# Where the empty instruction runs, when a bank may be borrowed, and how the plan prices a fold: one change to a two-layer SSM-convolution and gated-MLP kernel

## The chip, the cores and the metric

The kernel runs on one core of one Trainium2 chip. The metric is device microseconds of one execution, taken as the median of several. The engines are called by the names of the profile: PE (TensorE, matrix products), PEld (its weight loads), ACT (ScalarE), DVE (VectorE), POOL (GpSimd) and SP (SyncE, which issues DMAs).

## The reference, cut to what matters

```python
x = A_q                                            # 1 x 2048 x 576, bf16
x = x + A(layernorm(x), A_k, A_v, shift_k, ssm_k, ssm_D)
x = x + B(layernorm(x), w_gate, w_up, w_down)
x = x + A(layernorm(x), ...)                       # the same A and B again
x = x + B(layernorm(x), ...)

# A: kv = causal 4-tap convolution of k with shift_k, times v
#    y  = irfft(rfft(kv) * rfft(ssm_k))[:2048] + kv * ssm_D      (along the sequence)
#    returns q * y                                 (q is the normalised x)
# B: (gelu(x @ w_gate) * (x @ w_up)) @ w_down      (576 -> 4608 -> 576)
```

The convolution y does not depend on x, so both layers use the same y. The MLP B is run for each of the two layers and is nearly all of the arithmetic.

## The kernel before, in words

**Units and visits.** The 2048 rows are cut into 4 chunks of 512. A unit is one layer of one chunk; there are 8, in the order (layer 0, chunk 0), (0, 1), (1, 0), (1, 1), (0, 2), (0, 3), (1, 2), (1, 3), numbered 0 to 7. The 4608 features are cut into three phases of 12 tiles of 128. A visit is one unit in one phase, so there are 24, which this text numbers 0 to 23. Visits 0 to 2 belong to unit 0, 3 to 8 to units 1 and 2 in turn, 9 to 14 to units 3 and 4, 15 to 20 to 5 and 6, and 21 to 23 to unit 7.

**One visit.** First the gate and up products: 12 tiles (`gu`, L1081), each 18 matmuls of 64 weight rows by 512 columns, gate on one half of the array's rows and up on the other, so that two run side by side. Each tile is then gated into `hT`: GELU on ACT and the product on DVE, in one of two ways. Either ACT does the GELU alone and DVE multiplies straight out of the accumulator bank (L1673, L1674), or ACT also copies the up half out (L1664, L1665) and DVE multiplies two bf16 tiles (L1666); the second way frees the bank without DVE. It is taken when `hurry()` holds or convolution work for DVE is queued, and ACT is free by the plan. After the 12 tiles comes the down product (`dn`, L1735) for 4 rows of 128 tokens, two rows at a time (`two_rows`).

**Half rows and the empty instruction.** A `dn` row is accumulated into the two banks of a pair, one for each half of the 576 columns. In step 0, array rows 0 to 63 feed the first bank and 64 to 127 the second; in step 1 it is the other way round. Between the steps stands `conv.hold`: an instruction that does nothing, but is made to depend on the accumulator, so that it waits for the last matmul of step 0 and the first matmul of step 1 waits for it. It sits in ACT's instruction queue (L1110) and shows in the profile as an EVENT_SEMAPHORE. The forward and inverse transforms of the convolution (`cps`, L310) use the same two steps through `both_steps`. In `two_rows` the order by hand is: 10 features of the first row, 9 of the second, the last 2 of the first, the last 3 of the second (all step 0), then step 1 of both. The last features come late because their `hT` is late.

**Banks.** The accumulator memory is used as four double banks. Three go round in turn: `pr` hands out the next to each gate/up tile and each down row. The fourth belongs to the convolution. When it is taken, the convolution may borrow the next of the three (`conv.alt`); a row or tile that comes after then gets the bank behind it. `bank_at` holds when each is free by the plan.

**The plan.** The order on every engine is fixed when the kernel is built. A set of clocks (`t.pe`, `t.dve`, `t.act`) is advanced by constants (`C_GU`, `C_DN`, `C_FOLD` and so on). After each tile, and after every second pair of matmuls in a down product, `fill` runs what is due: step 1 of convolution transforms that were opened (`run_open`), loads, additions of finished rows (`late`), convolution products on DVE (`run_v`, allowed up to a limit ahead of `t.pe`), and new transforms on PE (`run_p`). The convolution of chunk m ends in two `fold`s on DVE (L559, L560: four operations each), after which the inverse transform can run. Until the last row of chunk 1's y is planned (`hurry()`), transforms may also run between gate/up tiles; afterwards only inside down products.

`turn_row` (L1097) transposes a normalised row on PE when it would be late by DMA; `opened` takes a bank for a row; `evict` queues the addition of a finished row to x (L1752, L1765, L1771, L1773).

Of the kernel before, what the change touches and what calls it, by code (L numbers as in the profile page):

```python
# [22 lines left out]
HW = 288  # L23
# [5 lines left out]
C_GU, C_DN = 1.944, 0.245  # L29
# [4 lines left out]
C_P0, C_P1, C_AC = 1.28, 1.35, 0.7  # L34
C_TT, C_ST, C_BN, C_NORM, C_HT, C_GELU, C_EVA, C_EVD, C_YH = 0.74, 0.80, 0.47, 0.62, 0.615, 0.51, 0.56, 0.72, 0.7
C_HB = 0.345
C_FOLD = 0.38
C_TURN, DRAIN = 0.0, 0.35
LAG = 0.25
AHEAD = 2.0  # L40
# [94 lines left out]
class Conv:  # L135
# [177 lines left out]
    def both_steps(self, outs, terms):  # L313

        ps = self.ps()
        self.half_rows(outs(ps), terms, 0)
        self.hold(ps)
        yield
        self.half_rows(outs(ps), terms, 1)
        return ps  # L320

# [73 lines left out]
    def step(self, m, kv=None, loaded=False):  # L395
# [155 lines left out]
        def fold(sg):  # L551

            def run():
                if sg == 0:
                    w["free"] = self.acp.tile([P, 2, D], BF16, tag="ac", name="w")[:, 0, :]
                for plane in range(2):
                    a, b = z[plane, 0, sg][:], z[plane ^ sg, 1, sg][:]
                    up, down = (sg, sg + 2) if sg == 0 or plane else (sg + 2, sg)
                    nc.vector.tensor_tensor(out=w["free"], in0=a, in1=b, op=ALU.add)  # L559
                    nc.vector.tensor_tensor(out=a, in0=a, in1=b, op=ALU.subtract)  # L560
                    w[up, plane], w[down, plane], w["free"] = w["free"], a, b

                def fin(when):
                    for part in range(2):
                        mark(("z", sg, part), when + LAG)
                    if sg:
                        self.z_at[m] = when
                return fin
            return run
# [18 lines left out]
        for sg in range(2):  # L588
            self.V.append((now, 4 * C_FOLD, fold(sg)))
        ab = {}  # L590
# [141 lines left out]
    def run_p(self):  # L732
        t = self.t
        if not self.Pq:
            return False
        ready, cost, run = self.Pq[0]
        self.cur = 0 if self.ps_free[0] <= t.pe else 1
        if self.cur and ready() <= t.pe and self.ps_free[0] <= t.pe + (0.3 if self.between else 0.0):
            self.cur = 0
            t.pe = max(t.pe, self.ps_free[0])  # L740
        if ready() > t.pe or self.ps_free[self.cur] > t.pe or self.cur and (self.alt is None or self.alt_at() > t.pe):
            return False
        self.Pq.popleft()
        run = run()
        if next(run, "whole") == "whole":
            t.pe += cost
            if self.cur:
                self.borrowed(self.slot(), self.ps_free[1])
            return True
        self.ps_free[self.cur] = NEVER  # L750
        t.pe += cost / 2
        self.open.append((t.pe + DRAIN, cost / 2, run, self.cur, self.slot()))
        return True

    def run_open(self, now):
# [10 lines left out]
def ssm_geglu_kernel(ctx, tc, A_q, A_k, A_v, A_shift_k, A_ssm_k, A_ssm_D, B_x, B_w_gate, B_w_up,  # L766
                     B_w_down, out):
    nc = tc.nc
# [7 lines left out]
    FP = FT // NP  # L776
# [13 lines left out]
    t = Pace()  # L790
# [10 lines left out]
    def bank(n, name, shape=(P, 2, 512), dt=F32):  # L801
        return banks[n].tile(list(shape), dt, tag="pr", name=name)
# [12 lines left out]
    def add_late():  # L815
        ready, n, run = late.popleft()
        run()
        bank_at[n % 3] = t.on_dve(C_EVD, ready) + 0.15

    bank_at, was = [0.0] * 3, [0.0]  # L820

    def pr(name):
        while late and taken[0] - late[0][1] >= 2:
            add_late()
        taken[0] += 1
        was[0] = bank_at[taken[0] % 3]
        bank_at[taken[0] % 3] = NEVER
        return bank(turn[(taken[0] - 1) % 3], name)
# [11 lines left out]
    conv = Conv(tc, ctx, t, gwork, xtp, A_k, A_v, A_shift_k, A_ssm_k, A_ssm_D, ident,  # L840
                lambda *form: bank(turn[3], "cps", *form), ypool)
# [265 lines left out]
        conv.ps_free[0] = xn_at[ui]  # L1107
        xn_done[ui] = j + 1

    conv.hold = lambda ps: nc.scalar.keepalive_nop([nc.scalar.lower_ap(ps[:, :, 0:HW])])  # L1110
    conv.slot = lambda: taken[0] % 3
    conv.borrowed = bank_at.__setitem__
    conv.alt_at = lambda: bank_at[(taken[0] + 1) % 3]
# [66 lines left out]
    with tc.manual_schedule():  # L1180
# [6 lines left out]
        with ExitStack() as es:  # L1187
# [40 lines left out]
            ps = bank(3, "ps")  # L1228
# [3 lines left out]
            held = {}  # L1232
# [355 lines left out]
            order = plan.order({"DVE": 1.9, "ACT": 3.3, "PE": 3.0, "POOL": 3.0, "SP": 4.5})  # L1588
# [19 lines left out]
        hurry = lambda: (1, RT - 1) not in conv.y_at  # L1608
# [4 lines left out]
        for at, (wb, ph, ui, first, final) in enumerate(visits):  # L1613
# [32 lines left out]
            gone = deque([0.0] * 2, maxlen=2)  # L1646
            conv.alt = None
            for fi in range(FP):
                n, gi = divmod(wb * FP + fi, FG)
# [40 lines left out]
            def opened(j):  # L1690
                if j not in accs:
                    accs[j] = pr("dn"), taken[0]
                return accs[j]

            def row(j):
# [27 lines left out]

            def two_rows(j):

                order = ([(0, 0, fi) for fi in range(FP - 2)] + [(1, 0, fi) for fi in range(FP - 3)] +
                         [(0, 0, fi) for fi in range(FP - 2, FP)] + [(1, 0, fi) for fi in range(FP - 3, FP)] +
                         [(n, 1, fi) for n in range(2) for fi in range(FP)])
                for k, (n, step, fi) in enumerate(order):
                    acc, mine = opened(j + n)  # L1730
                    wn = wd[2 * wb + fi // WT][:, fi % WT, :]
                    lhs = hT[:, fi, (j + n) * P:(j + n + 1) * P]
                    for g in range(2):
                        r = slice((step ^ g) * HK, (step ^ g) * HK + HK)
                        nc.tensor.matmul(acc[:, g, 0:HW], lhsT=lhs[r], rhs=wn[r, g * HW:(g + 1) * HW],  # L1735
                                         start=step == 0 and fi == 0, stop=step == 1 and fi == FP - 1)
                    if step == 0 and fi == FP - 1:
                        conv.hold(acc)
                    t.pe += C_DN / 2
                    if step == 1 and fi == FP - 1:  # L1740
                        evict(j + n)
                    elif k % 2:
                        conv.alt = other
                        fill(t.pe + 1.5, True, conv.left > 0)

            def evict(j):
# [30 lines left out]

            conv.alt = other
            two_rows(0)
            if wb == NWB - 1:  # L1780
                conv.alt = None
                row(2)
                row(3)
            else:
                two_rows(2)
# [3 lines left out]
@with_exitstack  # L1789
def kernel(  # L1790
    ctx: ExitStack,
    tc: tile.TileContext,
    A_q: bass.AP,
    A_k: bass.AP,
    A_v: bass.AP,
    A_shift_k: bass.AP,
    A_ssm_k: bass.AP,
    A_ssm_D: bass.AP,
    B_x: bass.AP,
    B_w_gate: bass.AP,  # L1800
    B_w_up: bass.AP,
    B_w_down: bass.AP,
    out: bass.AP,
):
    ssm_geglu_kernel(tc, A_q, A_k, A_v, A_shift_k, A_ssm_k, A_ssm_D, B_x, B_w_gate, B_w_up,
                     B_w_down, out)
# [30 lines left out]
```

## Time and profile before

| what | value |
|---|---|
| median of 3 runs | 913.42 us (913.37 to 913.92) |
| the profiled execution | 913.37 us |
| its span, first to last instruction | 911.5 us |
| matmuls | 10451, busy 904.0 us |
| VectorE busy | 565.1 us |
| ScalarE busy | 363.2 us |
| GpSimd busy | 146.8 us |
| granted TensorE clock | 1.000 |

The profiled execution is 1.9 us longer than its span, and within 0.05 us of the median. Matmuls are pipelined: a recorded matmul is longer than the time by which it moves the next one, so a busy PE can still be losing time. In a timeline, rows that follow one another on an engine are merged: start, length, engine, line, operation, count, and in brackets the idle time before it with what ended it.

### The profile page before, as it was taken

The numbers are of one execution on the slowest core, as the hardware profiler recorded it, in microseconds if no ns is written. First come the engines' busy times: TensorE is split into PE (matmuls) and PEld (weight loads), VectorE is DVE, ScalarE is ACT, GpSimd is POOL, SyncE is SP. The second block draws the span as 40 slices with busy tenths as digits, with TensorE's granted clock in tenths as the row PEclk, the third lists the DMA queues.
The fourth block names the chain that finished last, engine by engine and source line by source line (L and its number), as shares of the span: only waits on it lengthen the run. The fifth ranks groups of instructions, "written<-read, shape, count | busy, mean of one in ns | idle before, by whom it ended". The sixth has DMA issues, their size and how long they took to land.

```text
span 911.5 us, 24246 instructions
## 1 busy us (share of the span) xinstructions
PE 904.0 (99%) x10451; PEld 600.2 (66%) x10451; DVE 565.1 (62%) x1129; ACT 363.2 (40%) x675; POOL 146.8 (16%) x311
## 2 busy tenths in 40 slices
PE   9999999999999999999999999999999999999998
PEld 7757656466576675765766757757757657667666
DVE  8888985885789886677888843553332334433332
ACT  7785445735425356354244223451121224321211
POOL 5533003220113012230023001220000002100000
PEclk9999999999999999999999999999999999999999
DMA  9999977449619604974934702772720820777630
GB/s 247 307 250 275 249 164 144 113 126 235 201 53 231 142 2 79 271 186 106 247 121 117 167 16 58 129 137 60 142 79 2 157 79 13 143 176 180 136 101 27
DMA packets 125839, 129.12 MB, mean 142 GB/s; under 512 B 40866, under 2 KB 118051, under 8 KB 125732
## 3 DMA queue, kind: packets, MB, share of 16 engines
q1 hardware_dynamic: 116706, 92.63, 47.8%
q0 software_dynamic: 8880, 34.36, 11.4%
q8 instruction: 81, 1.33, 0.6%
q10 hardware_dynamic: 146, 0.59, 0.2%
q14 instruction: 26, 0.21, 0.1%
HBM read 106.91 MB, written 11.80 MB: 130 GB/s over the span
## 4 chain that ended last, share of the span: by engine, by line
PE 94%; DVE 4%; ACT 1%; issue 1%; POOL 0%; ACTq 0%
PE gu L1081 58%; PE dn L1735 29%; PE cps L310 2%; PE ps L284 2%; DVE kvt L255 1%; PE dn L1701 1%; DVE kvt L261 1%; DVE kc L633 0%; PE ps L1317 0%; DVE hT L1666 0%; DVE cd L334 0%; PE ps L1452 0%; PE ps L1081 0%; DVE hh L633 0%; POOL rstd L1537 0%
## 5 line engine op out<-in xcount | busy, mean ns | idle before, releaser
L1081 PE MATMUL gu<-xnT,wgu 64*128 64x512 bf16 x5148 | 561.0, 376 | 1.1 <-DVE hT L1674 0.9
L1081 PEld LDWEIGHTS <-wgu 64*128 64x128 bf16 x5220 | 293.5, 94 | 262.3 <-issue 2.3
L1735 PE MATMUL dn<-wd,hT 64*128 64x288 bf16 x4512 | 294.6, 283 | 0.8 <-ACTq L1110 0.4
L1735 PEld LDWEIGHTS <-hT 64*128 64x128 bf16 x4512 | 253.3, 94 | 28.7 <-issue 1.6
L1673 ACT ACTIVATE ga<-gu 128x512 f32<-128x512 f32 x175 | 104.4, 597 | 318.9 <-PE gu L1081 312.7
L1674 DVE TENSOR_TENSOR hT<-ga,gu 128x512 bf16<-128x512 f32 x175 | 120.0, 686 | 172.5 <-ACT ga L1673 172.0
L1664 ACT ACTIVATE ga<-gu 128x512 bf16<-128x512 f32 x111 | 66.2, 597 | 148.4 <-PE gu L1081 140.6
L1666 DVE TENSOR_TENSOR hT<-ga 128x512 bf16<-128x512 bf16 x112 | 46.9, 421 | 54.7 <-ACT ga L1665 54.7
L1665 ACT CAST ga<-gu 128x512 bf16<-128x512 f32 x111 | 64.4, 580 | 0.0
L911 POOL TENSOR_SCALAR means<-s 128x1 f32<-128x1 f32 x28 | 16.9, 606 | 245.1 <-DVE x_c L1765 216.8
L1773 DVE TENSOR_TENSOR x_c<-x_c,dn 128x576 f32<-128x576 f32 x32 | 23.9, 751 | 26.3 <-PE dn L1735 26.2
L1771 DVE SCALAR_TENSOR_TENSOR x_c<-dn,means,x_c 128x576 f32<-128x576 f32 x28 | 22.8, 815 | 24.5 <-PE dn L1735 24.4
L927 POOL TENSOR_TENSOR rstd<-ve,neghalf_t 128x1 f32<-128x1 f32 x56 | 34.9, 623 | 4.7
L329 ACT ACTIVATE eo<-cps 128x576 f32<-128x576 f32 x40 | 25.6, 657 | 21.3 <-PE cps L310 16.7
L346 DVE TENSOR_TENSOR prod<-prod 128x576 bf16<-128x576 bf16 x64 | 29.3, 458 | 2.2
L1752 DVE TENSOR_TENSOR xn<-x_c,dn 128x576 bf16<-128x576 f32 x15 | 11.3, 753 | 26.0 <-PE dn L1735 23.6
L633 DVE TENSOR_TENSOR kc<-ab,cd 128x288 bf16<-128x288 f32 x64 | 25.5, 451 | 0.0
L444 POOL DMA_DIRECT2D kr<-Kd x20 | 11.0, 552 | 85.9 <-DVE prod L345 85.9
L911 POOL TENSOR_SCALAR nm<-s 128x1 f32<-128x1 f32 x28 | 7.9, 281 | 94.8 <-DVE x_c L965 94.7
L919 ACT ACTIVATE junk<-x_c,nm 128x576 bf16<-128x576 f32 x28 | 21.5, 767 | 4.0 <-POOL nm L911 3.5
L955 ACT ACTIVATE yh<-y,rstd 128x576 f32<-128x576 bf16 x28 | 21.2, 768 | 2.3 <-PE dn L1735 1.4
L449 POOL DMA_DIRECT2D hr<-Hd x32 | 17.6, 551 | 21.4 <-DVE prod L345 19.9
(180 smaller groups left out, 629.9 us busy)
## 6 DMA issues: line engine op xcount, KB each, us to landing
wgu<-in_B_w_gate_dram SPq DMA_DIRECT2D x45, 576.0 KB, 6.0
wd<-in_B_w_down_dram SPq DMA_DIRECT2D x30, 864.0 KB, 6.5
wgu<-in_B_w_up_dram SPq DMA_DIRECT2D x45, 512.0 KB, 9.0
hr<-Hd POOLq DMA_DIRECT2D x32, 288.0 KB, 4.7
kr<-Kd POOLq DMA_DIRECT2D x24, 288.0 KB, 4.5
Kd<-kc POOLq DMA_DIRECT2D x12, 288.0 KB, 5.1
k<-in_A_k_dram POOLq DMA_DIRECT2D x3, 1008.0 KB, 10.9
wgu<-in_B_w_up_dram SPq DMA_DIRECT2D x45, 64.0 KB, 7.9
```

What stands on the lines that cost most here:

```text
L329: nc.scalar.activation(out=eo[:], in_=ps[:, :, 0:HW], func=ACT.Copy, scale=scale)
L346: nc.vector.tensor_tensor(out=dst[:, cols], in0=pr[:, 0, cols], in1=pr[:, 1, cols], op=ALU.subtract if part == 0 else ALU.add)
L633: nc.vector.tensor_tensor(out=into[k][:, plane, cols], in0=a, in1=b, op=op)
L911: nc.gpsimd.tensor_scalar(out=v["nm"][:], in0=v["s"][:], scalar1=-1.0 / D, scalar2=None, op0=ALU.mult)
L927: nc.gpsimd.tensor_tensor(out=v["rstd"][:], in0=ve[:], in1=neghalf_t[:, 0:1], op=ALU.pow)
L1081: nc.tensor.matmul(cols(pair[:, s, :]), lhsT=w[r0:r0 + HK, k, gi * P:(gi + 1) * P], rhs=cols(xnT[r0:r0 + HK, blk_of[k], :]), start=(k == 0 ...
L1664: nc.scalar.activation(out=ga[:, 0, :], in_=pair[:, 0, :], func=ACT.Gelu_apprx_tanh)
L1665: nc.scalar.copy(out=ga[:, 1, :], in_=pair[:, 1, :])
L1666: nc.vector.tensor_tensor(out=hT[:, fi, :], in0=ga[:, 0, :], in1=ga[:, 1, :], op=ALU.mult)
L1673: nc.scalar.activation(out=ga[:], in_=pair[:, 0, :], func=ACT.Gelu_apprx_tanh)
L1674: nc.vector.tensor_tensor(out=hT[:, fi, :], in0=ga[:], in1=pair[:, 1, :], op=ALU.mult)
L1735: nc.tensor.matmul(acc[:, g, 0:HW], lhsT=lhs[r], rhs=wn[r, g * HW:(g + 1) * HW], start=step == 0 and fi == 0, stop=step == 1 and fi == FP - 1)
```

## The change

Seven edits, all in how the kernel is ordered; nothing of what is computed changes.

1. `hold` is no longer always in ACT's queue: it goes to DVE's when the plan's ACT clock is later than both its DVE and its PE clock. It returns the time at which the plan takes it to be done.
2. Step 1 of a convolution transform is not due before that time (`run_p` keeps the later of it and the drain time); step 1 of a down row moves the plan's PE clock to it.
3. In `two_rows`, the number of features of the second row that go ahead of the first row's last two is no longer always 9. For the first pair of rows it is worked out from the planned time of the last `hT` (0 to 9); for the second pair it is 0.
4. After `hurry()` has ended, the convolution may borrow one of the three banks only in the second pair of rows of a down product. The last visit's second pair (`row`) borrows none, as before.
5. Taking a bank for a row moves the plan's PE clock to the time when that bank is free.
6. `C_FOLD`, the planned cost of one fold operation, is 0.46 instead of 0.38.
7. `both_steps` hands the time from `hold` on to `run_p`.

```diff
-C_FOLD = 0.38
+C_FOLD = 0.46
@@ both_steps
         self.half_rows(outs(ps), terms, 0)
-        self.hold(ps)
-        yield
+        yield self.hold(ps)
         self.half_rows(outs(ps), terms, 1)
@@ run_p
-        if next(run, "whole") == "whole":
+        held = next(run, "whole")
+        if held == "whole":
...
-        self.open.append((t.pe + DRAIN, cost / 2, run, self.cur, self.slot()))
+        self.open.append((max(t.pe + DRAIN, held), cost / 2, run, self.cur, self.slot()))
@@ ssm_geglu_kernel
-    conv.hold = lambda ps: nc.scalar.keepalive_nop([nc.scalar.lower_ap(ps[:, :, 0:HW])])
+    def hold(ps):
+
+        eng = nc.scalar if t.act <= max(t.dve, t.pe) else nc.vector
+        eng.keepalive_nop([eng.lower_ap(ps[:, :, 0:HW])])
+        return min(t.act, max(t.dve, t.pe)) + 0.15
+    conv.hold = hold
@@ opened
                     accs[j] = pr("dn"), taken[0]
+                    t.pe = max(t.pe, was[0])
@@ two_rows
-                order = ([(0, 0, fi) for fi in range(FP - 2)] + [(1, 0, fi) for fi in range(FP - 3)] +
-                         [(0, 0, fi) for fi in range(FP - 2, FP)] + [(1, 0, fi) for fi in range(FP - 3, FP)] +
+                held = {}
+                some = math.ceil((gone[-1] + 0.5 - t.pe) * 2 / C_DN) - (FP - 1)
+                some = max(0, min(FP - 3, some)) if j == 0 else 0
+                order = ([(0, 0, fi) for fi in range(FP - 2)] + [(1, 0, fi) for fi in range(some)] +
+                         [(0, 0, fi) for fi in range(FP - 2, FP)] + [(1, 0, fi) for fi in range(some, FP)] +
                          [(n, 1, fi) for n in range(2) for fi in range(FP)])
                 for k, (n, step, fi) in enumerate(order):
                     acc, mine = opened(j + n)
+                    if step == 1 and fi == 0:
+                        t.pe = max(t.pe, held[n])
...
                     if step == 0 and fi == FP - 1:
-                        conv.hold(acc)
+                        held[n] = conv.hold(acc)
                     t.pe += C_DN / 2
                     if step == 1 and fi == FP - 1:
                         evict(j + n)
                     elif k % 2:
-                        conv.alt = other
+                        conv.alt = other if hurry() or j == 2 else None
                         fill(t.pe + 1.5, True, conv.left > 0)
```

## The prediction

> **What bounds the kernel now.** The page first: how busy each engine is.
>
> ```profile
> PE 904.0 (99%) x10451; PEld 600.2 (66%) x10451; DVE 565.1 (62%) x1129; ACT 363.2 (40%) x675; POOL 146.8 (16%) x311
> ```
>
> PE is the bound. The change removes no matmul, so all it can win is time in which PE waits. To size that I need PE's pace without waits: the chain in order of time late in the run, and a window over nine whole visits.
>
> ```profile
> 861.18 11.76 PE dn L1735 x192
> 872.94 23.31 PE gu L1081 x216
> ...
> 580.44:896.07 315.63, 315.63 (x3675) 1.00 0.50 107
> ```
>
> A visit without waits is 23.31 + 11.76 = 35.07 us, and nine of them, 315.63 us, lose nothing. So from 580 us on there is nothing to win; the visits that carry convolution work are what matters. The same rows give the unit for measuring a wait: two matmuls run side by side, so a gate/up pair takes 23.31/108 = 0.216 us and a down pair 11.76/96 = 0.1225 us; transforms (also 288 columns) are taken at the down pair's pace. A wait is then the start of a group minus the start of the group before it and its pairs. This is more than the idle time in the list of waits, because the modelled end of a matmul lies beyond the start of the next:
>
> ```profile
> PE gu L1081 <- DVE hT L1674: 0.9, 1, 0.9
> PE dn L1735 <- ACTq L1110: 0.4, 1, 0.4
> PE cps L310 <- ACTq L1110: 0.4, 1, 0.4
> PE dn L1735 <- DVE x_c L1771: 0.3, 2, 0.2
> ```
>
> Four kinds of wait, and each is named by a part of the change: a gate late behind DVE (the folds), two empty instructions (L1110), and a down row waiting for an addition to free its bank. All that PE loses in this region is small: 0.2% of 913.42 us is 1.83 us, about what a measurement of this kernel can tell from no change.
>
> **Folds priced at 0.46 (edit 6).** Visit 12, gate/up:
>
> ```profile
> 518.98 7.95 PE L1081 MATMUL gu<-xnT,wgu 64*128 64x512 bf16 x72
> 523.32 0.45 DVE L559 TENSOR_TENSOR w<-yb 128x576 bf16<-128x576 bf16 x1
> 526.76 0.46 DVE L560 TENSOR_TENSOR yb<-yb 128x576 bf16<-128x576 bf16 x1
> 527.14 2.09 DVE L1674 TENSOR_TENSOR hT<-ga,gu 128x512 bf16<-128x512 f32 x3
> 527.87 1.04 PE L1081 MATMUL gu<-xnT,wgu 64*128 64x512 bf16 x8 [0.94 <-DVE hT L1674]
> ```
>
> 36 pairs from 518.98 end at 526.75; PE goes on at 527.87: 1.12 us lost. Eight fold operations stand in front of the gate of the second tile, whose bank PE needs; they start 0.49 us apart ((526.76 - 523.32)/7) where the plan has 0.38. By the plan's constants, counted from the end of the first tile: gate at 1.67, the two shifts (0.78) to 2.45 (in the trace the tile ends 9 pairs after 518.98, at 520.92, and the first fold starts at 523.32, 2.40 later), one fold (four operations) to 3.97, the second to 5.49; the limit is C_GU + FAR = 5.54, so both go in. At 0.46 the first ends at 4.29 and the second would at 6.13: it has to wait for the next `fill`. Then convolution work is still queued, so the second tile takes the way that frees its bank from ACT, and its gate goes ahead of the second fold. At the measured 0.49 the second fold ends near 527.6, the third tile's gate 0.7 later at 528.3, and PE wants that bank at 518.98 + 5 x 1.94 = 528.7. So nothing is late next, by 0.4 us. I take -1.1; the ends are -1.12 and 0, should the folds fall elsewhere.
>
> **The empty instruction on the earlier engine, and step 1 not before it (edits 1, 2, 7).** First row, in visits 3 and 0:
>
> ```profile
> 183.63 0.82 DVE L334 TENSOR_TENSOR cd<-eo 128x288 f32<-128x288 f32 x2
> 183.64 0.65 PE L1735 MATMUL dn<-wd,hT 64*128 64x288 bf16 x8
> 184.37 0.82 DVE L633 TENSOR_TENSOR kc<-ab,cd 128x288 bf16<-128x288 f32 x2
> 184.62 0.65 ACT L329 ACTIVATE eo<-cps 128x576 f32<-128x576 f32 x1 [1.73 <-DVE cd L334]
> 184.71 0.42 PE L1735 MATMUL dn<-wd,hT 64*128 64x288 bf16 x4 [0.42 <-ACTq L1110]
> ...
> 65.12 0.74 PE L310 MATMUL cps<-ht,T 64*128 64x288 bf16 x4
> 65.69 0.42 PE L1735 MATMUL dn<-wd,hT 64*128 64x288 bf16 x4
> 66.17 0.59 ACT L1664 ACTIVATE ga<-gu 128x512 bf16<-128x512 f32 x1
> 66.49 0.30 PE L310 MATMUL cps<-ht,T 64*128 64x288 bf16 x2 [0.38 <-ACTq L1110]
> ```
>
> Visit 3: four pairs from 183.64 end at 184.13, PE goes on at 184.71: 0.58 us. The empty instruction was queued behind an eviction (L329) that itself waited for DVE to read the last one (cd). Three things now work on this: DVE may be chosen; in the first pair of rows there is one transform at a time, so evictions rarely queue; and more of the second row stands between the first row's step 0 and step 1. Ends: -0.58 and 0; I take -0.45, nearer the full wait, because any one of the three would do.
>
> Visit 0: two pairs from 65.69 end at 65.94, PE goes on at 66.49: 0.55 us, a transform's step 1 behind a GELU. Edit 2 leaves step 1 until the plan has the empty instruction done, with rows in between. The 0.33 us before it (two pairs from 65.12 end at 65.36, next at 65.69) is a borrowed bank, which edit 4 leaves alone here since `hurry()` holds. What is late next is the last gate, so I take -0.45 of ends -0.88 (both waits) and 0.
>
> Behind an empty instruction in DVE's queue stand additions and `cross` operations of the transforms; they wait until step 0 is drained. Its own execution costs nothing:
>
> ```profile
> L1110 ACTq EVENT_SEMAPHORE  x150: 17/17/17, 43.5 to 899.2; - x150
> ```
>
> **Banks, and the order of rows (edits 3, 4, 5).** Visits 4 and 9, the second pair of rows:
>
> ```profile
> 225.17 1.16 PE L1735 MATMUL dn<-wd,hT 64*128 64x288 bf16 x16
> 225.63 0.81 DVE L1771 SCALAR_TENSOR_TENSOR x_c<-dn,means,x_c 128x576 f32<-128x576 f32 x1
> 226.50 0.67 PE L1735 MATMUL dn<-wd,hT 64*128 64x288 bf16 x8 [0.17 <-DVE x_c L1771]
> ...
> 407.29 1.16 PE L1735 MATMUL dn<-wd,hT 64*128 64x288 bf16 x16
> 408.63 0.65 PE L1735 MATMUL dn<-wd,hT 64*128 64x288 bf16 x7 [0.17 <-DVE x_c L1771]
> ```
>
> Eight pairs from 225.17 end at 226.15, next 226.50: 0.35 us, and from 407.29 likewise 0.36. Row 4 opens after 10 pairs of row 3 and gets a bank whose row is still being added. In the second pair row 4 now opens after 12 pairs, 2 x 0.1225 = 0.245 us later, and with nothing borrowed in the first pair it may get an older bank. Per visit -0.245 by the order alone, -0.35 at most: I take -0.5 for both, ends -0.7 and 0. Visit 8 is the same at row 3:
>
> ```profile
> 363.95:376.39 12.44, 1.03 (x8) 0.00 (x0) 1.21 (x2) 1.00 1.20 216
> ...
> 369.71 0.75 DVE L1752 TENSOR_TENSOR xn<-x_c,dn 128x576 bf16<-128x576 f32 x1
> 370.51 6.06 PE dn L1735 x96
> ```
>
> The first row is the transforms' part of that down product, 8 matmuls beside the 192 of the rows: 100 pairs at 0.1225 are 12.25 of its 12.44 us, so 0.19 is lost. The second half of the rows starts at 370.51, right after an addition ends at 370.46: a bank wait, which goes if nothing is borrowed before. -0.19, ends -0.19 and 0. Visit 7 loses 0.3 to 0.4 in pieces that I leave as they are.
>
> What is given back: borrowing moves next to the following visit's gate/up, which takes the bank after. In visits 3, 4, 7 and 9 that can cost a wait like the one of visit 4 (0.35 us) each, or none: ends 0 and +1.4; I take +0.3, as the additions of the second pair have more than a tile before their bank is wanted.
>
> The last features as soon as gated: in the quiet visits,
>
> ```profile
> 896.07 3.12 PE L1735 MATMUL dn<-wd,hT 64*128 64x288 bf16 x48
> 896.28 0.60 ACT L1673 ACTIVATE ga<-gu 128x512 f32<-128x512 f32 x1 [1.34 <-PE gu L1081]
> 896.91 0.69 DVE L1674 TENSOR_TENSOR hT<-ga,gu 128x512 bf16<-128x512 f32 x1 [1.25 <-ACT ga L1673]
> ```
>
> `hT` is done 1.53 us after the first down matmul. The plan has 1.53 + 0.5 margin: 17 pairs, so PE now wants it after 2.08 us rather than 20 pairs or 2.45. Still 0.55 us to spare, so nothing in ten visits. ACT is idle from 896.88 on, so the empty instruction stays with ACT there.
>
> **The sum.** -1.1 - 0.45 - 0.45 - 0.5 - 0.19 + 0.3 = -2.4 us, from the profiled execution's 913.37: 911.0 us; the median of the runs is 0.05 higher. With every wait gone, -1.12 - 0.58 - 0.88 - 0.7 - 0.19 = -3.5: 909.9. With the folds alone and the full +1.4 it is 913.7.
>
> **The rivals.** *A, the first inverse slips by a tile* (about the same). The plan's dearer folds make z later, 8 x 0.08 = 0.64 us, in visit 2 as well:
>
> ```profile
> 135.48 0.46 DVE L560 TENSOR_TENSOR yb<-yb 128x576 bf16<-128x576 bf16 x1
> 137.29 0.42 PE L374 MATMUL cps<-w,V 128*128 128x288 bf16 x2
> 155.53 0.76 DVE L1102 COPY xnT<-cps 128x1152 bf16<-128x1152 bf16 x1 [1.22 <-PE cps L1097]
> 157.03 0.38 PE L1081 MATMUL gu<-xnT,wgu 64*128 64x512 bf16 x2
> ```
>
> z is done at 135.94 and the inverse starts at 137.29, a tile boundary. One boundary later is 1.94 us; the chain through gate, square, norm and transposes ends at 156.29, and visit 3's gate/up starts at 157.03 without a wait, so 1.94 - 0.74 = 1.2 us would show: 912.2. For it: the boundary is decided by plan clocks that I cannot see. Against: 1.35 us of slack is more than 0.64.
>
> *B, the choice of engine gains nothing.* At 184.62 ACT starts an eviction of 0.65 us and PE is released at 184.71, 0.56 us before its end. So the empty instruction does not need ACT idle; it was held by the wait in front of it, while the plan compares clocks of busy time. If it then leaves both waits of L1110, the two terms of 0.45 go: 911.9. The Trainium skill (Advanced Engine Details and Errata, Sequencer Loop) says that engine instructions are put in a queue and control instructions start in the sequencer, so a busy engine need not hold one up; it speaks against choosing by busy clocks, and this trace agrees, with that 0.56 us.
>
> *C, trapped behind DVE* (slower). In the down products with convolution work DVE is the fuller engine, and it may be planned 1.5 us ahead of PE:
>
> ```profile
> 180.46:194.26 13.80, 13.38 (x30) 1.00 0.52 127
> 217.57:231.64 14.07, 12.23 (x30) 1.00 1.01 177
> ```
>
> These are DVE's busy times, 97% and 87%. An empty instruction sent to DVE stands behind `cross` operations and an addition (0.81) that wait for other things. If eight of those in visits 0, 3, 4, 7 and 9 wait 0.8 us each beyond their cover, that is +6.4; with the two terms of 0.45 not won, 913.4 - 1.5 + 6.4 = 918.3. It decides from 1.5 + 1.83 = 3.3 us of such waits on. Against: edit 2 plans around the wait, and the plan takes DVE only where its clock is the earlier.
>
> **How the numbers follow.** Forecast 0.56 (its own range 909.8 to 911.6), A 0.13, B 0.15, C 0.16. Faster by over 0.2% means under 911.59: the forecast, 0.56. Within 0.2%, up to 915.25, are A, B and a hundredth of C, where few empty instructions are caught: 0.29. Slower is the rest of C, 0.15. For 8 in 10 the range runs from all waits gone, 909.9 (909.8 with a tenth for the median and its spread), over A and B to the folds alone with new bank waits, 913.7 (913.8 likewise); what it leaves out is C.
>
> **What would show it.** Right: the wait of `gu` on L1674 gone and a gate between the two folds; no PE wait on an empty instruction; the two waits on L1771 gone or under 0.1; visits 13 to 22 still 35.07 us apart from their transforms. Wrong: waits of PE on DVE's queue at the new `hold`; the first inverse after 139 us; a transform of chunk 3 that misses visit 9 and so delays unit 5; a new wait of `gu` on an addition at the end of visits 3, 4, 7 or 9.

## The result, and the profile after

The changed kernel takes 911.63 us (median of 20 executions, 911.20 to 912.47), the kernel before beside it 913.25 us (20 executions, 913.08 to 913.92). The ratio is 0.9981 with a 95% interval of 0.9974 to 0.9988: a real gain, 1.6 us, whose middle lies just inside the 0.2% that the prediction called hard to tell from no change. The profiled execution took 911.2 us, the lowest of its 20, with a span of 909.4 us. The span of before was 911.5 us.

The page of the kernel after, busy times; then the list of PE's waits in the same execution (the two of the prologue, which both kernels have, left out):

```profile
PE 903.0 (99%) x10451; PEld 601.1 (66%) x10451; DVE 563.2 (62%) x1128; ACT 365.4 (40%) x678; POOL 146.4 (16%) x311
...
PE dn L1746 <- ACT ga L1670: 0.4, 1, 0.4
PE gu L1081 <- DVE x_c L1782: 0.3, 1, 0.3
PE cps L310 <- ACT ga L1670: 0.2, 1, 0.2
```

PE does the same 10451 matmuls. All four kinds of wait that the prediction quoted from the kernel before are gone: the gate behind the folds, the two empty instructions, the additions before a down row. Three others stand there now. The quiet visits are as they were, nine of them in 315.63 us (a window over the same work as in the prediction):

```profile
578.31:893.94 315.63, 315.63 (x3676) 1.00 0.50 107
```

To compare kernels I measure a wait as the prediction does, start to start against the pace of 0.216 us for a gate/up pair and 0.1225 us for a down or transform pair, and add up all that exceed 0.04 us from 40 us on. Before, the sum is 5.35 us; after, 3.19. The difference, 2.16, is near that of the spans, 2.1, but not the same stretch: the last addition starts 2.25 us earlier (905.90 for 908.15), and 0.2 us of that is lost again behind it, where only the last store is left; why, isn't shown. About 1.2 us of either sum stand in both kernels: the steps from 64-row to 128-row matmuls and back (last section), and 0.28 us at the entry into the main loop. This sum is called the loss below. It is of the one execution that was profiled.

**The folds (visit 12).** Timeline of PE and DVE, after:

```profile
517.85 12.48 PE L1081 MATMUL gu<-xnT,wgu 64*128 64x512 bf16 x114
...
523.53 0.42 DVE L1671 TENSOR_TENSOR hT<-ga 128x512 bf16<-128x512 bf16 x1
523.87 0.45 DVE L558 TENSOR_TENSOR w<-yb 128x576 bf16<-128x576 bf16 x1
...
525.34 0.46 DVE L559 TENSOR_TENSOR yb<-yb 128x576 bf16<-128x576 bf16 x1
525.71 0.42 DVE L1671 TENSOR_TENSOR hT<-ga 128x512 bf16<-128x512 bf16 x1
526.05 0.45 DVE L558 TENSOR_TENSOR yb<-yb 128x576 bf16<-128x576 bf16 x1
```

A gate (L1671) stands between the first fold (523.87 to 525.80) and the second (from 526.05), another ahead of both, and PE runs 114 matmuls without a break. The 1.12 us are gone.

**Visit 0.** Timelines of PE and ACT, after, 65 to 68 us:

```profile
65.50 1.16 PE L1746 MATMUL dn<-wd,hT 64*128 64x288 bf16 x16
67.10 0.67 PE L1746 MATMUL dn<-wd,hT 64*128 64x288 bf16 x8 [0.45 <-ACT ga L1670]
...
65.21 0.79 ACT L919 ACTIVATE junk<-x_b,means 128x576 bf16<-128x576 bf16 x1
...
65.98 0.60 ACT L1669 ACTIVATE ga<-gu 128x512 bf16<-128x512 f32 x1
66.46 0.59 ACT L1670 CAST ga<-gu 128x512 bf16<-128x512 f32 x1
```

No empty instruction holds PE here any more, but eight pairs from 65.50 end at 66.48 and PE goes on at 67.10: 0.63 us lost. The second down row wants the bank of the last gate/up tile. That bank is free when ACT has copied it (66.46 + 0.59 = 67.05), and ACT did a squaring of a later chunk's row (L919) first. Together the visit loses 0.346 (at 65.38, the same copy of the tile before) + 0.628 + 0.101 + 0.050 = 1.13 us, where before it lost 0.324 + 0.554 + 0.155 + 0.124 = 1.16.

**Visit 3, and visits 4 and 9.** Timeline, after, with the last columns as above:

```profile
190.99 2.61 PE L1746 MATMUL dn<-wd,hT 64*128 64x288 bf16 x40
...
193.08 0.81 DVE L1782 SCALAR_TENSOR_TENSOR x_c<-dn,means,x_c 128x576 f32<-128x576 f32 x1
193.94 1.02 PE L1081 MATMUL gu<-xnT,wgu 64*128 64x512 bf16 x7 [0.34 <-DVE x_c L1782]
...
226.31 1.89 PE L1746 MATMUL dn<-wd,hT 64*128 64x288 bf16 x28
228.18 0.30 PE L310 MATMUL cps<-v,T 64*128 64x288 bf16 x2
```

The 0.58 us at visit 3's first row is gone. At its end 20 pairs from 190.99 end at 193.44, and visit 4's first gate/up tile starts at 193.94, when an addition has freed its bank: a new 0.50. Visit 4's 0.344 is now 0.155 (14 pairs from 226.31 end at 228.03; the transform starts at 228.18), visit 9's 0.353 is 0.157. Visit 8's 0.19 is gone, and visit 7's three pieces (0.355 together) are one of 0.074.

### The profile page after: what moved, and what is told of

Read it like the earlier page. It is cut to its first block, busy times and chain, and to the rows that moved or that the text cites. A ratio compares the mean times of both kernels' runs of the same rounds, so it can differ in the third digit from the quotient of the medians.

```text
span 909.4 us, 24248 instructions
## 1 busy us (share of the span) xinstructions
PE 903.0 (99%) x10451; PEld 601.1 (66%) x10451; DVE 563.2 (62%) x1128; ACT 365.4 (40%) x678; POOL 146.4 (16%) x311
## 4 chain that ended last, share of the span: by engine, by line
PE 94%; DVE 4%; ACT 1%; issue 0%; POOL 0%; ACTq 0%; DVEq 0%
PE gu L1081 59%; PE dn L1746 29%; PE cps L310 2%; PE ps L284 2%; DVE kvt L255 1%; PE dn L1707 1%; DVE kvt L261 1%; PE ps L1322 0%; DVE kc L632 0%; DVE hT L1671 0%; PE ps L1457 0%; PE ps L1081 0%; DVE hh L632 0%; POOL rstd L1542 0%; PE ps L1235 0%
## 5 line engine op out<-in xcount | busy, mean ns | idle before, releaser
L1671 DVE TENSOR_TENSOR hT<-ga 128x512 bf16<-128x512 bf16 x114 | 47.9, 421 | 55.6 <-ACT ga L1670 55.4
L919 ACT ACTIVATE junk<-x_c,nm 128x576 bf16<-128x576 f32 x28 | 21.5, 768 | 3.2 <-POOL nm L911 2.6
L333 DVE TENSOR_TENSOR ab<-eo 128x288 f32<-128x288 f32 x40 | 16.1, 453 | 8.3 <-ACT eo L328 6.4
```

What stands on the lines that cost most here:

```text
L1671: nc.vector.tensor_tensor(out=hT[:, fi, :], in0=ga[:, 0, :], in1=ga[:, 1, :], op=ALU.mult)
```

## The experiments

Each kernel ran beside the kernel before on the same chip. The numbers:

| kernel | median us | before | ratio to before, 95% interval | loss us |
|---|---|---|---|---|
| before | | | | 5.35 |
| after | 911.63 | 913.25 | 0.9981 (0.9974 to 0.9988) | 3.19 |
| after, again | 911.46 | 913.04 | 0.9983 (0.9974 to 0.9991) | 3.17 |
| fold only | 912.16 | 913.32 | 0.9986 (0.9978 to 0.9995) | 4.18 |
| hold only | 915.88 | 913.32 | 1.0030 (1.0019 to 1.0042) | 7.38 |
| borrow only | 911.98 | 913.32 | 0.9986 (0.9978 to 0.9995) | 4.70 |
| order only | 912.86 | 913.32 | 0.9996 (0.9987 to 1.0005) | 5.04 |
| after without hold | 911.14 | 913.37 | 0.9974 (0.9963 to 0.9984) | 3.50 |
| after, always ScalarE | 911.24 | 913.37 | 0.9974 (0.9964 to 0.9985) | 3.17 |
| hold, always ScalarE | 915.33 | 913.37 | 1.0018 (1.0009 to 1.0028) | 6.78 |
| visit 0 borrows late | 912.86 | 913.37 | 0.9994 (0.9985 to 1.0003) | 5.15 |
| visit 3 borrows nothing | 911.26 | 913.04 | 0.9980 (0.9971 to 0.9989) | 3.42 |
| calm last gates | 909.90 | 913.04 | 0.9966 (0.9954 to 0.9979) | 2.14 |
| calm, and the rest | 909.68 | 913.36 | 0.9962 (0.9948 to 0.9976) | 1.89 |

**Each part alone.** First the price of a fold (edit 6) on the kernel before:

```diff
-C_FOLD = 0.38
+C_FOLD = 0.46
```

> Kernel before with C_FOLD = 0.46 alone. My theory: visit 12's gate goes between the two folds, the 1.12 us wait of gu goes and nothing else moves: -1.0 to -1.2 us. Rival: the plan shifts elsewhere as well, above all the first inverse in visit 2, and gives some back: -0.5 or less.

It measured -1.16 us by the medians. The loss went from 5.35 to 4.18, and every other wait of the main loop stayed within 0.02 us of before. DVE's timeline of this kernel:

```profile
524.64 0.46 DVE L560 TENSOR_TENSOR yb<-yb 128x576 bf16<-128x576 bf16 x1
525.02 0.42 DVE L1666 TENSOR_TENSOR hT<-ga 128x512 bf16<-128x512 bf16 x1
525.35 0.45 DVE L559 TENSOR_TENSOR yb<-yb 128x576 bf16<-128x576 bf16 x1
```

A gate between the two folds, as the prediction worked it out. The first inverse stays on its tile boundary (137.13 us; 137.29 before).

Then the empty instruction with all that goes with it (edits 1, 2 and 7) on the kernel before:

```diff
-    conv.hold = lambda ps: nc.scalar.keepalive_nop(...)
+    def hold(ps):
+        eng = nc.scalar if t.act <= max(t.dve, t.pe) else nc.vector
+        eng.keepalive_nop([eng.lower_ap(ps[:, :, 0:HW])])
+        return min(t.act, max(t.dve, t.pe)) + 0.15
...
+                    if step == 1 and fi == 0:
+                        t.pe = max(t.pe, held[n])
```

> Kernel before with the choice of engine for the empty instruction and its planned time handed on (edits 1, 2, 7) alone. My prediction: -0.9 us, the waits on the empty instruction in visits 0 and 3 both smaller. Rival (from the trace after): in visit 0 PE then meets the bank of the last gate/up tile, which ScalarE frees at the same time whatever the empty instruction does, so only visit 3 gains: -0.3 to -0.6 us. Rival B: nothing, within 0.2 us.

It is slower, by 2.56 us, which none of the three answers foresaw. Timelines of PE and DVE of this kernel, at the end of visit 0, in visit 2 and at its end:

```profile
82.14 0.42 PE L1743 MATMUL dn<-wd,hT 64*128 64x288 bf16 x4
82.73 0.81 DVE L1779 SCALAR_TENSOR_TENSOR x_c<-dn,mv,x_c 128x576 f32<-128x576 f32 x1
83.59 2.12 PE L1081 MATMUL gu<-xnT,wgu 64*128 64x512 bf16 x18 [1.03 <-DVE x_c L1779]
...
140.38 0.42 PE L373 MATMUL cps<-w,V 128*128 128x288 bf16 x2
...
151.20 0.68 PE L1097 MATMUL cps<-ident,xn 128*128 128x128 bf16 x9
151.81 2.62 PE L1743 MATMUL dn<-wd,hT 64*128 64x288 bf16 x40
154.75 0.42 PE L1743 MATMUL dn<-wd,hT 64*128 64x288 bf16 x4 [0.31 <-DVEq L1113]
...
157.78 0.68 PE L1097 MATMUL cps<-ident,xn 128*128 128x128 bf16 x9
```

A new wait of 1.21 us at the end of visit 0 (83.59 less 82.14 and two pairs): the addition that frees the bank stands behind convolution products on DVE. The first inverse starts one tile later, at 140.38. PE then transposes three rows (L1097; the middle one, at 155.10, is left out here) where it was two, each 151.81 - 151.20 = 0.61 us. Once PE waits for an empty instruction in DVE's queue, 0.475 us. Visit 0 has the same four losses as the changed kernel (0.337, 0.629, 0.102, 0.050) and 0.11 us more at 74.99. Visit 3 passes without any wait, as the prediction had it, but visits 4, 7 and 9 lose more than before: 0.553, 0.648 and 0.557 us against 0.344, 0.355 and 0.353. In all the loss is up by 2.03 us; with the nine matmuls of the added transposition (0.51 us, the steps to it and back being in the loss) that makes 2.54, near the difference of the spans, 914.1 - 911.5 = 2.6.

Borrowing in second pairs only, and a bank moving the plan's clock (edits 4 and 5), on the kernel before:

```diff
                     accs[j] = pr("dn"), taken[0]
+                    t.pe = max(t.pe, was[0])
...
-                        conv.alt = other
+                        conv.alt = other if hurry() or j == 2 else None
```

> Kernel before with borrowing in second pairs of rows only after the first visits, and the plan's PE clock moved to a row's bank (edits 4, 5). My theory: the waits of rows on additions in visits 4, 8 and 9 go (0.9 us together) and the end of visit 3 gets a new wait of gate/up on an addition (0.5 us): -0.2 to -0.7 us. Rival: the new wait in visit 3 comes from another edit and this one alone gives -0.9 us.

It measured -1.34 us, more than either answer foresaw. The bank waits of visits 4, 7, 8 and 9 are gone, with 0.139 and 0.140 us left in visits 4 and 9. Visit 3's 0.58 is gone too, but 0.399 and 0.148 stand at its end. The profile also has 0.72 us in visit 0:

```profile
80.65 0.55 PE L1736 MATMUL dn<-wd,hT 64*128 64x288 bf16 x5
81.64 0.41 PE L1736 MATMUL dn<-wd,hT 64*128 64x288 bf16 x3 [0.43 <-issue]
```

PE stops here between the two matmuls of a pair (five before the stop, three after it), and the profile shows nothing that it waits for ("issue"). This belongs to the execution rather than to the edits: the profile caught one with a span of 910.8 us, where 6 of the kernel's 11 executions have 909.9. Without the 0.72 the loss would be 3.98, 1.4 us under that of before, and 1.4 is also what lies between 909.9 and the commonest span of the kernel before beside it, 911.3.

Visit 12's fold wait also fell here, from 1.12 to 0.73, with nothing about folds changed.

The order of the features (edit 3) alone:

```diff
-                order = ([(0, 0, fi) for fi in range(FP - 2)] + [(1, 0, fi) for fi in range(FP - 3)] + ...
+                some = math.ceil((gone[-1] + 0.5 - t.pe) * 2 / C_DN) - (FP - 1)
+                some = max(0, min(FP - 3, some)) if j == 0 else 0
+                order = ([(0, 0, fi) for fi in range(FP - 2)] + [(1, 0, fi) for fi in range(some)] + ...
```

> Kernel before with the order of rows and features alone (edit 3). My theory: row 4 opens 0.245 us later, so visits 4 and 9 lose 0.1 instead of 0.35 us each, and the empty instruction of the first row has more cover in visit 3: -0.5 to -0.9 us. Rival: the row meets the same late addition, or a new wait on the last gate: within 0.3 us of before.

It measured -0.46 us, between the two answers, and the interval of its ratio holds 1. In visits 4 and 9 the bank waits go from 0.344 and 0.353 to 0.111 each, near the 0.245 us that the later opening of row 4 was worked out to give. A further 0.100 per visit appears at the next transform. The empty instruction of visit 3 no longer holds PE, though nothing about it changed. In its place stand 0.318 (a bank), 0.092 and 0.139 us, 0.55 together.

By the medians the four parts add up to -1.16 + 2.56 - 1.34 - 0.46 = -0.40 us, and the whole is worth -1.62. They are not independent, so the next runs take parts away from the whole.

**The whole without the hold.** The changed kernel with edits 1, 2 and 7 undone:

> The changed kernel with the empty instruction as before (edits 1, 2, 7 undone; folds, order of rows and borrowing kept). Theory after the single edits: handing on the planned time moves work for the worse and the other edits only make up for it, so without it the three single gains add up: -1.2 - 1.3 - 0.5 = -3.0 us from the kernel before, 1.3 us faster than the changed kernel. Rival: the edits overlap in the same waits, and it comes out like the changed kernel, -1.3 to -1.9 us, with the wait on the empty instruction in visit 0 (0.55 us) back.

It is 2.23 us faster than before, between the two answers; the sign of the second, visit 0's wait on the empty instruction, is there. On the same chip the changed kernel with ScalarE only (next run) takes 911.24 us for its 911.14. The profile caught the slowest of its eight executions (span 909.8, the shortest have 909.2), so the 3.50 of the table is high. So in company these three edits gain nothing, and their harm alone (2.56 us) does not appear either: the changed kernel's first inverse starts at 137.04. PE's waits in this kernel, from the list:

```profile
PE cps L310 <- ACTq L1110: 0.6, 2, 0.4
```

One of the two is visit 0's old wait (0.556 us lost), the other is at 191.09 in visit 3 (0.408, with 0.142 at its end). So visit 0 loses 1.17 us with the old hold and 1.13 with the new one, visit 3 0.55 and 0.50.

**Only ScalarE.** The changed kernel, with the choice of engine alone taken out:

```diff
-        eng = nc.scalar if t.act <= max(t.dve, t.pe) else nc.vector
+        eng = nc.scalar
```

> The changed kernel with the empty instruction always in ScalarE's queue; the plan and the order on TensorE are the same to the last instruction. Rival B (the choice of engine gains nothing): within 0.3 us of the changed kernel, -1.3 to -1.9 us from before. My prediction's term (the choice saves a wait in visit 0 or 3): 0.4 us or more slower than the changed kernel. Rival C (it traps): faster than the changed kernel by 0.4 us or more.

It measured 911.24 us, 0.22 under the changed kernel's repeat, which ran on another chip. The order of PE's work is the same, and so are its waits: the list has the same three lines as that of the changed kernel, with the same numbers. The loss is 3.17 against 3.19: that 19 of 150 empty instructions went to DVE moved no wait.

The same taken out of the hold alone, on the kernel before (edits 2 and 7, always ScalarE):

> Kernel before with the planned time of the empty instruction handed on (edits 2, 7), but the instruction always in ScalarE's queue. If the time handed on makes edits 1, 2, 7 slower by themselves (it moves the plan, and with it the borrowed banks and the first inverse): +2.0 to +3.0 us, as with the choice of engine. If VectorE's queue is the cause: within 0.5 us of before.

Still slower than before, by 1.96 us, just under the first answer's range, with 1.11 us lost at the end of visit 0 (83.39), the later inverse and the third transposition; only the wait for DVE's queue is missing. So most of the harm comes from the time handed on to the plan, and DVE's queue adds some half a microsecond (915.88 against 915.33). Whether step 1's later due time or the clock that a down row moves does it wasn't separated.

**Is it the borrowed bank that costs visit 0?** The changed kernel, with no borrowing in the first 25 steps of a first pair while `hurry()` holds:

```diff
-                        conv.alt = other if hurry() or j == 2 else None
+                        conv.alt = other if (hurry() and k > 24) or j == 2 else None
```

> The changed kernel, but in the first pair of rows nothing is borrowed in the first 25 steps, in visits 0 and 1 as well (k > 24). Theory: in visit 0 the borrowed bank is what makes PE wait 0.35 us and then gives row 2 the bank of the last gate/up tile (0.63 us); without it both go: -0.6 to -0.9 us from the changed kernel. Rival: PE waits there for the last gate anyway and gains less than 0.3 us, or the first transforms come later and the first inverse slips a tile: slower by about 1 us.

It takes 912.86 us, 1.62 more than the changed kernel with ScalarE only on the same chip (911.24), whose waits are those of the changed kernel: slower, as the rival had it. Timeline of PE:

```profile
65.02 1.65 PE L1746 MATMUL dn<-wd,hT 64*128 64x288 bf16 x24
67.16 0.30 PE L310 MATMUL cps<-ht,T 64*128 64x288 bf16 x2 [0.48 <-DVEq L1113]
...
73.13 0.42 PE L1746 MATMUL dn<-wd,hT 64*128 64x288 bf16 x4
75.08 0.42 PE L1746 MATMUL dn<-wd,hT 64*128 64x288 bf16 x4 [1.52 <-DVE x_c L1782]
```

PE stops after 12 pairs, at 66.49, and goes on at nearly the same time as in the changed kernel, 67.16 in place of 67.10, now released by the empty instruction; and it loses 1.71 us at 75.08 to an addition. The empty instruction stands behind the product of the last gate (a DVE operation at 67.07), which waited for the same copy on ACT. The theory that the borrowed bank is the cause falls: whatever PE turns to near 66.5 us, it finds the same lateness.

**The changed kernel again**, for the spread on another chip:

> The changed kernel itself once more, on one chip with the next ones: -1.3 to -2.2 us from before, as measured; the yardstick for them.

It measured 911.46 us and the same waits.

**Is it the gates?** In each of these kernels ACT's queue has a squaring (L919) ahead of the last gate of visit 0. In that visit, the optional work of ACT is held off from the tenth gate/up tile until the tiles are done:

```diff
-        run_aq(min(limit, t.pe + 2.3))
+        if not calm[0]:
+            run_aq(min(limit, t.pe + 2.3))
...
+                calm[0] = at == 0 and fi >= FP - 3
```

> The changed kernel, but in visit 0 no squaring or summing (L900, L919) is put into ScalarE's queue from the tenth gate/up tile to the end of the tiles, so that the last gate is not behind them; they run later. Theory: it is ScalarE's late last gate that PE meets in visit 0 in every version, and with it gone the 0.35 and 0.63 us there shrink: 0.5 to 1.0 us faster than the changed kernel. Rival: the postponed statistics delay chunk 1 or the plan moves elsewhere: within 0.3 us, or slower.

Timelines of PE and ACT of this kernel:

```profile
65.14 1.16 PE L1749 MATMUL dn<-wd,hT 64*128 64x288 bf16 x16
...
66.37 1.16 PE L1749 MATMUL dn<-wd,hT 64*128 64x288 bf16 x16
...
64.87 0.60 ACT L1670 ACTIVATE ga<-gu 128x512 bf16<-128x512 f32 x1 [0.81 <-PE gu L1081]
65.36 0.58 ACT L1671 CAST ga<-gu 128x512 bf16<-128x512 f32 x1
65.83 0.79 ACT L919 ACTIVATE junk<-x_b,means 128x576 bf16<-128x576 bf16 x1
```

The last gate starts at 64.87 and not at 65.98, the squaring comes after it, and PE passes the whole stretch at its pace: the losses of 0.346, 0.628 and 0.101 us are gone and none came for them. The time is 909.90 us, 1.56 under the changed kernel's repeat on the same chip (1.27 by the lowest of each, 909.88 and 911.15), more than the 0.5 to 1.0 expected. The traces show 1.03 of it as loss (3.17 to 2.14), and the last addition starts 1.02 us earlier (904.85 for 905.87); another 0.2 us of the spans falls behind that addition. This shows the cause in visit 0: the down product wants the last gates' banks at once, and a squaring of 0.8 us was put in front of them.

**Visit 3's half microsecond.** It has been there in most versions: 0.58 before, 0.55 with the order or the borrowing alone, 0.55 in the whole without the hold, 0.50 in the changed kernel. Only the hold alone was free of it, and paid in visits 4, 7 and 9. The changed kernel without borrowing in visit 3's second pair:

```diff
-                        conv.alt = other if hurry() or j == 2 else None
+                        conv.alt = other if hurry() or j == 2 and at != 3 else None
```

> The changed kernel without borrowing in the second pair of rows of visit 3 alone; TensorE's order differs only by one transform that comes a few down matmuls later. If the new wait of gate/up at the end of visit 3 (0.50 us) is the price of borrowing there, it goes and the kernel is 0.3 to 0.5 us faster than the changed one. Rival: the addition is late because VectorE is full, whatever bank is taken: the same wait, within 0.2 us.

Timeline of PE and DVE at the end of visit 3:

```profile
191.41 0.30 PE L310 MATMUL cps<-ht,T 64*128 64x288 bf16 x2
...
192.15 1.90 PE L1746 MATMUL dn<-wd,hT 64*128 64x288 bf16 x28
193.38 0.81 DVE L1782 SCALAR_TENSOR_TENSOR x_c<-dn,means,x_c 128x576 f32<-128x576 f32 x1
193.86 1.48 PE L1081 MATMUL gu<-xnT,wgu 64*128 64x512 bf16 x12
```

Gate/up starts on pace (14 pairs from 192.15 end at 193.87) while the addition still runs, with a bank that does not need it. A transform waits 0.158 us at 191.41 instead. So the new wait came from the borrowing, 0.34 us net in this place. The medians (911.26 and 911.46) are too close to show it, and the loss of the profiled execution is even higher, 3.42: it has 0.224 us at 81.00, before anything in the plan differs, and 0.431 at 409.86 where the changed kernel had 0.157, and these 0.27 us take back most of the 0.34.

**Both, with ScalarE only.**

> The changed kernel with the last gates of visit 0 not behind other work of ScalarE (as in the run before that did so), nothing borrowed in the second pair of visit 3, and the empty instruction always on ScalarE. If the waits left are each a loss by themselves: the three waits of visit 0 (0.35, 0.63 and 0.10 us) and the 0.50 us at the end of visit 3 are both gone, some 0.3 us of the latter come back as a wait of a transform or a first gate/up tile near 191 us, and the time is 0.2 to 0.5 us under that of the run with the calm last gates alone (909.4 to 909.7 us where the kernel before gives 913.1). If the wait of visit 3 only changes its place: within 0.2 us of that run (909.7 to 910.1 us).

Timeline of PE at the end of visit 3, and further on in visit 9:

```profile
190.81 1.89 PE L1749 MATMUL dn<-wd,hT 64*128 64x288 bf16 x28
192.52 3.85 PE L1081 MATMUL gu<-xnT,wgu 64*128 64x512 bf16 x34
...
402.21 1.16 PE L1749 MATMUL dn<-wd,hT 64*128 64x288 bf16 x16
403.47 0.30 PE L310 MATMUL cps<-v,T 64*128 64x288 bf16 x2
```

It took 909.68 us, 0.22 under the kernel with the calm gates, on the border between the two answers. In the trace the waits of visits 0 and 3 are both gone (0.156 us remain in visit 3), and a transform in visit 9 waits 0.28 us at 403.47 that had waited 0.15. Of the 1.89 us that this kernel still loses, 1.2 are no waits.

## Why the prediction was right or wrong, point by point

The predicted 911.0 us stands against 911.2 in the profiled execution and 911.63 in the median; it forecast a gain of over 0.2%, and the gain is 0.18% (0.12 to 0.26): the direction and the mechanism of most of it held, and the size fell short. One of the signs that it named for being wrong did come, a new wait of gate/up on an addition at the end of visit 3. Term by term, in the profiled executions:

| term | predicted us | measured us |
|---|---|---|
| folds, visit 12 | -1.1 | -1.12 |
| empty instruction, visit 3 | -0.45 | -0.58 |
| empty instruction, visit 0 | -0.45 | -0.03 |
| banks and order, visits 4 and 9 | -0.5 | -0.39 |
| bank, visit 8 | -0.19 | -0.19 |
| visit 7 | 0 | -0.28 |
| given back | +0.3 | +0.50, all in visit 3 |
| sum | -2.4 | -2.1 |

That the sums lie within 0.3 us is in part luck: 0.42 us that visit 0 did not give, 0.20 more given back and 0.11 less in visits 4 and 9 are set off by 0.28 in visit 7, which had no price, and 0.13 in visit 3.

**Folds.** Right in mechanism and size. The prediction put the second tile's gate between the folds; in the kernel with this edit alone it is so. In the changed kernel one gate stands ahead of both folds and the next one between them.

**Visit 0: the step that failed.** "What is late next is the last gate, so I take -0.45 of ends -0.88 (both waits) and 0." The last gate was named but priced at 0.4 of the wait. In fact it was late by all of it: with step 1 moved away, PE met the bank of the last gate tile 0.6 us later, and 0.03 us came out. The kernel before showed it already, on ACT:

```profile
65.41 0.79 ACT L919 ACTIVATE junk<-x_b,means 128x576 bf16<-128x576 bf16 x1
66.65 0.59 ACT L1665 CAST ga<-gu 128x512 bf16<-128x512 f32 x1
```

A squaring (L919) comes first, the GELU of the last tile follows at 66.17, its copy at 66.65, and the empty instruction stood behind that GELU. The step should have asked when the copy ends and what else needs it. The calm gates confirm it: with the squarings of that one place moved, 1.03 us of loss is gone. The kernel with the hold alone shows the same exchange, 1.12 us for 1.16.

**Visit 3.** The size was nearly right, the reason only in part. The hold alone does remove this wait, but so do the order alone and the borrowing alone, and in company the hold is not needed for it. With the order or the borrowing what goes at the first row comes back later in the same visit, 0.55 us without the hold and 0.50 with it, so that the net gain here is 0.08. The prediction counted the return separately, at 0.3 for four visits; it came in one visit, at 0.5. That this visit is the one where DVE is fullest (13.38 busy of 13.80 us in the prediction's row) fits, but is not shown to be the cause. Not borrowing in the second pair is what took 0.34 of it away.

**Banks and order.** Right for visit 8, 0.11 us too much for visits 4 and 9, where a transform of 0.15 us is late next. Visit 7 was left at nothing and won 0.28: its largest piece, 0.21 us of gate/up behind an addition (340.64), is a bank wait as in visits 4 and 9, and should have had a price. This made up for two thirds of what visit 0 lacked.

**Rival A**, a first inverse that slips a tile: its mechanism exists, but belongs to another edit. The dearer fold leaves the inverse where it was (137.13); the handed-on time of edits 2 and 7 moves it to 140.38 and buys a third transposition, in the kernel that has these edits alone. In the changed kernel it does not happen. Which of the other edits prevents it wasn't tried.

**Rival B**, the choice of engine gains nothing: confirmed, 3.17 against 3.19 us of loss with and without it, and likewise for all three edits of the hold (911.14 us without them). The time it gave, 911.9, counted visit 3's wait as staying; the other edits removed that one. The Trainium skill (Advanced Engine Details and Errata, Sequencer Loop) says that the sequencer pushes an engine instruction into a queue and starts a control instruction in its own microcode. The trace is in line with that: the changed kernel sent 19 of them elsewhere by busy clocks, and no wait moved.

**Rival C**, trapped behind DVE: it does not occur in the changed kernel. Twice in other kernels PE waits for an empty instruction in DVE's queue, 0.475 us at 154.75 and 0.66 at 67.16: near the 0.8 that the prediction gave one case, but one of them in a kernel, not eight.

**The medians.** The profiled executions differ by 2.17 us, the medians by 1.62. The changed kernel's executions spread over 1.3 us, those of the kernel before over 0.8. Most of the changed kernel's spread lies inside its span, which goes from 909.4 us, that of the profile, to 910.4; half of the twenty executions have 909.7 or more. In all 21 executions of the kernel before that stand beside the repeat the span is 911.2 to 911.4, though on the chip of the first eight experiments it goes up to 912.6. The changed kernel's slowest, 912.47, has a span of 909.5 and lost its time outside it. No longer execution of the changed kernel itself was profiled, so what it loses isn't settled. Profiles of its variants that caught one show single stops of PE: 0.72 us at 81.64 with the borrowing alone and 0.224 at 81.00 in the kernel that borrows nothing in visit 3, both in the middle of a pair.

## What to carry to other kernels

Before a wait is counted as won, look at what the waiting instruction stood behind, and ask who else needs that; moving the instruction to another queue, or the work that waited, wins nothing while the work in front of it (here a squaring of 0.8 us ahead of the last gate) stays where it is. Parts of a plan don't add up: alone, these four came to -0.40 us, together to -1.62, and one that cost 2.6 us alone cost nothing in company, so a part is to be tried by taking it out of the whole as well. A planned duration that is too short (0.38 for a measured 0.49) can be worth as much as the re-arranging around it (1.1 us of 2.1), and is read off one row.

## What the runs showed of the hardware that was not expected

An empty instruction takes 17 ns in ACT's queue and 21 ns in DVE's, every time. From the source view of the changed kernel:

```profile
L1113 ACTq EVENT_SEMAPHORE  x131: 17/17/17, 43.3 to 897.0; - x131
L1113 DVEq EVENT_SEMAPHORE  x19: 21/21/21, 67.1 to 762.6; - x19
```

The list of waits understates a stop of PE: in the kernel with edits 1, 2 and 7 alone it shows 1.03 us at 83.59 where PE started 1.21 late, since the recorded end of the matmul before lies beyond the time at which the next could have started.

Going from matmuls of 64 rows to one of 128 rows costs PE a tenth of a microsecond each way here, with no wait in the list; what in the step takes it isn't shown. Timeline of PE, changed kernel, around a transposition:

```profile
149.84 2.12 PE L1746 MATMUL dn<-wd,hT 64*128 64x288 bf16 x32
151.89 0.68 PE L1097 MATMUL cps<-ident,xn 128*128 128x128 bf16 x9
```

Sixteen pairs from 149.84 end at 151.80, and the transposition starts at 151.89; the step back costs 0.10 as well. In the changed kernel there are eight such steps around the first inverse and the two transpositions, 0.78 us together, most of the 1.2 us of loss that no edit touched.
